# First two batches of an attention-and-MLP kernel: a new order, priced decoding, banks of their own for pooled values

## Chip, core and metric

The kernel runs on one core of one Trainium2 chip, in one launch. The metric is the device time of that launch in microseconds (us), lower is better. The engines are PE (matrix multiply, TensorE), DVE (VectorE), ACT (ScalarE), POOL (GpSimd) and SP, whose queue starts the transfers.

## What is computed

Eight batches j of eight heads, 576 tokens of 64 values each. Every head gets two attentions, and their sum goes through a layer that takes the maximum of three products:

```python
q_d, k_d, v_d = (t.reshape(B, H, 144, 4, 64).mean(axis=3) for t in (q, k, v))
out_up = np.repeat(sm_attn(q_d, k_d, v_d), 4, axis=2)      # pooled, every row repeated 4 times
scores = np.where(np.abs(i - j) < 4, scale * q @ k.T, -1e9)  # local
out_local = softmax(scores) @ v
x = (out_up + out_local)            # as 4608 tokens x 512
h = max(x @ w1, x @ w2, x @ w3)     # 512 -> 768
out = h @ w_out                     # 768 -> 512
```

q, k, v are float32, the weights are float64.

## The kernel before, in words

**Units of work.** A batch is a block j; n = 2j and 2j+1 are its halves of four heads (two pairs each). What of the 144 pooled positions goes beyond 128 is kept apart for all batches and makes a ninth block. A block's way: local and pooled attention give x, transposed (features on the partitions) in four tiles of 128x512, one per pair of heads; `transposes(j, c)` splits each into xhi (fp32r, cast by ACT) and xlo = x - xhi (DVE). `mlp_column(j, ft)` makes 128 of the 768 hidden values: 3 weights x 4 tiles x 3 products (xhi*whi, xhi*wlo, xlo*whi), 36 matmuls of 512 columns into three banks; then the maximum, then `mlp_out`. Blocks 2 to 7 do their local attention on DVE, POOL and ACT (products prod<-k,pq, sums of 1792 values, x<-pv).

**The first two batches.** Nothing can be multiplied by the weights until the first x is there. `dense(0)` and `dense(1)` therefore compute batches 0 and 1 by banded matmuls on PE: `band_load`, `wide_scores` or `band_scores`, softmax on ACT and DVE, `wide_values` or `band_values` (into banks given by PX), `band_sums` (pooled q and k), `pool_scores`, and `pooled_values`. ORDER names these steps in the order in which they are recorded: a letter (l load q and k, w load v, s scores, k pooled sums, v values, P pooled scores and softmax, V pooled values), then the half n, then the pair where it has one. FIRST, POOLED and PULL are their priorities.

**IN_PSUM.** Where it is True for n, the local values stay in their PSUM bank (stop=False) and `pooled_values` adds the pooled product onto them there. Since one pooled row is for four tokens, the moving operand is read four times: matmuls of 64x512, and of 64x16 for the rest. Then xhi is cast from the bank and xlo subtracted from it. Where it is False, `band_done` copies the local values to the tile x, the pooled product goes into a bank of its own as 64x144, ACT copies it to od, and `transposes` adds the two on DVE into t (t<-x,od) before the cast and the subtraction:

```python
elif c in blk["band"]:
    xs = new([P, FAC * P], tag="t", bufs=3, name=f"xs_{j}_{c}")
    tt(xs..., blk["band"][c], od, ALU.add)
    act.copy(hi, xs)
    tt(lo, xs, hi.bitcast(F32), ALU.subtract)
```

Before, batch 0 (n=0 and 1) is summed in PSUM, batch 1 takes the way just quoted.

**Weights.** `weight_piece` fetches one of 24 pieces of 128x512 float64 (524 KB) raw into the tile that STAGE or STAGE_OUT names for it (tiles that are otherwise wo, hh or pv), and decodes it in four steps: a cast to 16 bit of the top part (hqk<-hh, hqk<-wo or hqk<-pv, on ACT or DVE), SCALAR_TENSOR_TENSOR on DVE (shift and or, in place), whi (or the hi half of wo) by a cast on ACT, and wlo = value - whi on DVE or POOL. Three pieces serve one MLP column.

**The order.** All calls are recorded by `Recorder.add`; `place` is a list scheduler that keeps a model of each engine's time. `price` gives each call's duration, and the constants LAG, LAG0, MLP, PE_LAG, BANK_LAG, HOP, LOAD, SPARE and PATIENCE_DVE give what it adds for hand-overs, due times and choices between engines. Calls that two engines can do (`tt`, `copy`) go where the model has them done earlier. Each engine's queue is then emitted in that fixed order at one line, L639 (L643 after the change), so all instructions carry this line and are told apart by their tiles. Where the model has PE waiting up to the time KEEP_TO, `warm` puts fillers in: matmuls with the constant tile prod as both operands, 128x448 bf16, into a bank that is free (KEEP_UP and GUARD decide how densely).

Of the kernel before, what the change touches and what calls it, by code (L numbers as in the profile page):

```python
# [15 lines left out]
HALF = (BF16, F16, U16)  # L16
# [22 lines left out]
QW2 = D - 6  # L39
NW2 = 9  # L40
QT2 = NW2 * QW2
EXPS = (1, 2, 0, 2)
GEO = ("wide", "small")
EPS = 1e-9
QS = 1.0 / 128.0
QB = 1.0 / 8.0
XBUFS = 5
LAG = 317.941
LAG0 = 109.942
MLP = 2180.474  # L50
PE_LAG = 2614.299
BANK_LAG = 2600.0
SEG = FAC * P
NDENSE = 2
FIRST = (13.78, -82.74, 12.12, 93.98)
DENSE_SPARE = 182.496
POOLED = (-29.04, -8.81, 69.1, 12.11)
IN_PSUM = (True, True, False, False)
PULL = (-884.46, -2751.93, 13232.89, 22753.07)
PX = (['pq', 'pm'], ['pm', 'pm'], ['pq', 'pa'], ['pa', 'pa'])  # L60
VHOMES = ('k', 'pv', 'wlo4', 'whi4')
HOMES = ('whi2', 'whi3', 'whi2', 'pv', 'whi5', 'whi5', 'wlo4', 'wlo4')
STAGE = ('hh3', 'hh1', 'wo4', 'hh4', 'pv', 'hh3', 'wo5', 'wo5', 'wo4', 'pv', 'hh4', 'wo0', 'hh4', 'wo1', 'wo0', 'pv', 'hh5', 'hh4')
STAGE_OUT = ('hh4', 'hh1', 'hh0', 'hh5', 'hh4', 'hh5')
ALIGNED = ("prod", "pv", "hqk", "hv", "pd", "pt", "qkT", "k", "v", "q", "qd", "kd", "traw", "vd", "tq", "th")
JOINT = 0
JOINT_LAG = 3170.373
W_ENGINES = ("POOL",)
S_ENGINES = ("DVE",)
C_ENGINES = ("DVE",)  # L70
# [27 lines left out]

ENGINES = ("PE", "DVE", "ACT", "POOL", "SP")
DONE_NS = {"PE": 230.0, "DVE": 150.0, "ACT": 190.0, "POOL": 200.0}  # L100
SPARE = 1994.467
PATIENCE_DVE = 187.71
PATIENCE = {"PE": 0.0, "DVE": 142.18, "ACT": 0.0, "POOL": 0.0, "SP": 0.0}
LANES = 8
RING = 128
# [6 lines left out]
PHASE = 2200.0  # L112
KEEP = 0.352
EASY = 0.0
ORDER = ('l0 s00 k00 l1 w1 k01 w0 s01 v01 v00 k10 s11 s10 k11 v10 v11 P0 V0 P1 V1', 'l0 k00 s0 w0 v0 l1 k01 k10 w1 k11 s1 v1 P0 V0 P1 V1')
TAGS = ('pm', 'pm', 'pa', 'pa')
GUARD = 0.015
KEEP_UP = 0.137
KEEP_TO = 53544.303
HOP = 684.824  # L120
STEP = 451.011
LOAD = 8107.482
SWITCH = {("R", "P"): 120.0, ("P", "R"): 110.0, ("P", "T"): 25.0, ("T", "P"): 93.0, ("t", "P"): 90.0, ("P", "t"): 90.0, ("B", "P"): 96.0, ("M", "P"): 100.0, ("P", "M"): 20.0, ("R", "T"): 10.0, ("T", "R"): 5.0, ("R", "M"): 91.0, ("T", "M"): 93.0, ("M", "R"): 300.0, ("M", "T"): 305.0, ("M", "B"): 0.0, ("B", "M"): 96.0, ("B", "R"): 120.0, ("t", "R"): 90.0, ("R", "t"): 95.0, ("t", "M"): 90.0, ("t", "B"): 90.0, ("t", "T"): 90.0, ("T", "t"): 90.0, ("M", "t"): 100.0}
COLD = 1.9

# [109 lines left out]
class Recorder:  # L235
# [48 lines left out]
    def add(self, forms):  # L284
# [17 lines left out]
        o.group = self.step + next(iter(forms))[:2]  # L302
        if "PE" in forms and self.lag in (LAG, MLP):
            o.lag, o.margin = PE_LAG, BANK_LAG
        elif self.lag == MLP:
            o.lag = 0.0
# [27 lines left out]
    def price(self, eng, method, args, kw):  # L334

        out = kw["out"] if "out" in kw else args[0]
        n = elems(out)
        src = [a for a in args[0 if "out" in kw else 1 :] if is_ap(a)] + [v for k, v in kw.items() if is_ap(v) and k not in ("out", "accum_out")]
# [30 lines left out]
        if eng == "DVE":  # L369
            if method == "memset":  # L370
                return 60.0 + 0.3 * n, False
            if method == "transpose":
                return 100.0 + 1.045 * n, False
            if method == "tensor_reduce":
                return 66.0 + 1.045 * elems(src[0]), False
            if method in ("tensor_scalar", "tensor_scalar_mul", "tensor_scalar_add", "reciprocal", "tensor_copy"):
                fast = not any(psum) and not self.psum(out)
                return (125.0 if method == "reciprocal" else 140.0 if n == TAIL else 72.0) + n * (0.53 if fast else 1.045), fast and method != "reciprocal"
            return (185.0 if n == HH * NO * FAC else 62.0) + 1.045 * n, big >= 2
        if eng == "ACT":  # L380
            if n <= D and list(out.ap)[0][1] == D and any(psum):
                return 165.0 + 0.9 * n, False
            return 0.833 * n + (58.0 if any(psum) else 100.0) + 90.0 * ptrs + (93.0 if "accum_out" in kw else 0.0), False
        if eng == "POOL":
            if method == "memset":
# [265 lines left out]
def local_global_attention_maxout_kernel(ctx: ExitStack, tc: tile.TileContext, q, k, v, qt_dense, kt_dense, qt_pool, kt_pool, qkt_tail, v_win0, v_win1, v_tail, w_in, w_out, ident_d, mask_d, band_d, out):  # L651
# [463 lines left out]
    def wide_scores(n, pr, tag):  # L1115
# [16 lines left out]
        for i in range(2):  # L1132
            part = sm[:, :, i]
            if i < EXPS[n]:
                dve.tensor_reduce(out=mx[:, i], in_=sps[i], axis=AX.X, op=ALU.max, negate=True)
# [107 lines left out]
    def pair_operands():  # L1243
# [17 lines left out]
        for c in range(NCC):  # L1261
# [3 lines left out]
            for f in range(FAC):  # L1265
                pe.transpose(ps[:, f], x[:, f], ident)
            rec.lag = LAG
            tag, bufs = (("hv", 1), ("pt", 1), ("x", XBUFS), ("x", XBUFS))[c]
# [195 lines left out]
    def block(j):  # L1464
        rec.spare = SPARE
        for n in (2 * j, 2 * j + 1):
            with at(100.0 * n, LAG):
                attention(n)
        rec.spare = 0.0

    def turn(j):
        with at(-200.0, LAG0 if j < 2 else LAG):
            for c in range(NCC):
# [16 lines left out]
    for j in range(B + 1):  # L1490
# [8 lines left out]
        if 6 < n < 2 * B:  # L1499
            rec.spare = SPARE  # L1500
            with at(100.0 * n, LAG):
                begin(n)
# [3 lines left out]
    state["blk", B]["h"] = [None] * NFT  # L1506
    with at(100.0 * 2 * (B + 1), LAG):
        xt = pair_operands()
    with at(-100.0, MLP):
        joint_in(xt)  # L1510
# [52 lines left out]
```

## Time and profile before

| | us |
|---|---|
| median of 3 runs (lowest, highest) | 703.22 (702.65, 704.92) |
| the profiled execution | 701.49 |
| its span, first to last instruction | 699.7 |
| PE busy | 690.2 (99%) |
| DVE busy | 611.5 (87%) |
| ACT busy | 417.2 (60%) |
| POOL busy | 376.9 (54%) |

How to read it: the span lies 1.8 us below the profiled execution's own time, and that lies 1.7 below the median. A matmul's busy time overlaps that of its neighbours (a 128x512 lasts 0.39 us alone and comes every 0.23 in a row), so on PE the distance from start to start counts. The same holds, less strongly, for ACT and DVE. A filler counts as PE work. The wait in brackets in a timeline is the engine's idle time ahead of that instruction, with the instruction or transfer that ended it.

### The profile page before, as it was taken

Reading aid. Unit: us, or ns where it says so; the run is one execution under the profiler, and the core shown is the slowest. Engines: PE = TensorE matmul, PEld = TensorE weight load, DVE = VectorE, ACT = ScalarE, POOL = GpSimd, SP = SyncE. Lnnn points to the kernel's source line nnn. Section 1 sums busy time; section 2 is a strip of 40 time slices with the busy share of each in tenths; the row PEclk is TensorE's granted clock in tenths of the full one; section 3 lists DMA queues with packets and bytes.
Section 4 is the critical chain, followed back from the end, with each engine's and each line's share of the span. In section 5 each row is a group of like instructions: output and inputs, shape, how many; then the busy total and the mean of one; then the engine's idle time right before and its main releaser. Section 6 shows DMA issues by size and latency. Waiting matters only on the chain.

```text
span 699.7 us, 12779 instructions
## 1 busy us (share of the span) xinstructions
PE 690.2 (99%) x4350; PEld 547.8 (78%) x4350; DVE 611.5 (87%) x842; ACT 417.2 (60%) x1423; POOL 376.9 (54%) x590
## 2 busy tenths in 40 slices
PE   7999999999999999999999999999999999999997
PEld 4567887787887888778877887788788888888885
DVE  7987989999999999999999999999976398999620
ACT  5844466769578587857867665864866244334121
POOL 2102006899498888957757993975667013422000
PEclk9999999999999999999999999999999999999999
DMA  9994345765455555645374444441420010000012
GB/s 314 401 341 154 109 142 160 229 199 160 145 183 169 156 159 172 199 146 174 94 224 125 136 151 150 130 138 47 141 71 2 0 46 16 0 1 0 1 61 60
DMA packets 50180, 92.81 MB, mean 133 GB/s; under 512 B 5540, under 2 KB 19426, under 8 KB 50114
## 3 DMA queue, kind: packets, MB, share of 16 engines
q1 hardware_dynamic: 50114, 91.99, 41.7%
q8 instruction: 34, 0.56, 0.3%
q14 instruction: 32, 0.26, 0.1%
HBM read 82.53 MB, written 9.44 MB: 131 GB/s over the span
## 4 chain that ended last, share of the span: by engine, by line
PE 97%; DMA 1%; ACT 1%; DVE 0%; issue 0%; SPq 0%; ACTq 0%; DVEq 0%
PE pm L639 81%; PE pa L639 14%; PE pq L639 2%; DMA whi<-in_kt_dense_dram 1%; ACT pv L639 0%; SPq L639 0%; ACT y L639 0%; DVE xlo_0r L639 0%; DVE hh_0r L639 0%; DVE pa L639 0%; ACT xhi_0r L639 0%; ACT pd L639 0%; ACT dtail L639 0%; ACTq L1559 0%; DVE pdt L639 0%
## 5 line engine op out<-in xcount | busy, mean ns | idle before, releaser
L639 PE MATMUL pm<-xhi_0r,whi_0r 128*128 128x512 f32 x540 | 212.4, 394 | 0.0
L639 PE MATMUL pm<-xlo_0r,whi_0r 128*128 128x512 f32 x540 | 211.7, 393 | 0.0
L639 PE MATMUL pm<-xhi_0r,wlo_0r 128*128 128x512 f32 x540 | 211.6, 392 | 0.0
L639 ACT ACTIVATE pv<-v,sums 128x64 f32<-128x64 f32 x580 | 151.7, 413 | 22.5 <-POOL sums L639 10.4
L639 POOL TENSOR_TENSOR pv<-v,sums 128x256 f32<-128x256 f32 x233 | 138.7, 702 | 11.4 <-DVE x L639 8.7
L639 PE MATMUL pm<-wo_0r,hh_0r 128*128 128x512 f32 x576 | 138.7, 394 | 0.0
L639 PEld LDWEIGHTS pm<-wo_0r,hh_0r 128*128 128x128 f32 x576 | 106.6, 188 | 22.5 <-issue 1.3
L639 PEld LDWEIGHTS pm<-xhi_0r,whi_0r 128*128 128x128 f32 x540 | 101.5, 188 | 21.5 <-issue 1.1
L639 PEld LDWEIGHTS pm<-xlo_0r,whi_0r 128*128 128x128 f32 x540 | 101.4, 188 | 21.3 <-issue 0.7
L639 PEld LDWEIGHTS pm<-xhi_0r,wlo_0r 128*128 128x128 f32 x540 | 101.4, 188 | 21.0 <-issue 0.4
L639 DVE TENSOR_TENSOR prod<-k,pq 128x1792 f32<-128x1792 f32 x56 | 112.2, 2004 | 2.1 <-PE pa L639 1.8
L639 DVE TENSOR_REDUCE sums<-prod 128x28 f32<-128x1792 f32 x56 | 112.2, 2004 | 0.5
L639 DVE TENSOR_REDUCE x<-pv 128x256 f32<-128x1792 f32 x36 | 72.2, 2009 | 2.9 <-POOL pv L639 1.7
L639 POOL TENSOR_TENSOR pv<-pv 128x768 f32<-128x768 f32 (+1 forms) x40 | 62.2, 1555 | 3.6 <-ACT pv L639 1.8
L639 POOL TENSOR_TENSOR x<-whi_0r,wlo_0r 128x512 f32<-128x512 f32 x16 | 22.4, 1410 | 55.3 <-DVE x L639 28.4
L639 ACT COPY y<-pm 128x512 f32<-128x512 f32 (+1 forms) x50 | 28.9, 583 | 37.0 <-PE pm L639 32.9
L639 ACT CAST hh_0r<-pm 128x512 fp32r<-128x512 f32 x47 | 27.7, 589 | 38.8 <-DVE pm L639 37.8
L639 POOL TENSOR_TENSOR hv<-v 128x128 f32<-128x128 f32 (+1 forms) x52 | 25.1, 498 | 27.7 <-DMA v<-in_v_dram 13.0
L639 DVE TENSOR_TENSOR t<-pm,t 128x512 f32<-128x512 f32 x43 | 29.3, 680 | 10.4 <-PE pm L639 10.1
L639 ACT COPY pq<-q 128x256 f32<-128x256 f32 x56 | 22.1, 396 | 26.2 <-DVE prod L639 22.0
L639 DVE TENSOR_TENSOR pm<-pm,t 128x512 f32<-128x512 f32 x44 | 30.4, 690 | 4.9 <-PE pm L639 4.8
L639 DVE TENSOR_TENSOR hh_0r<-pm,hh_0r 128x512 fp32r<-128x512 f32 x47 | 31.9, 679 | 2.2 <-ACT hh_0r L639 2.0
(381 smaller groups left out, 1052.9 us busy)
## 6 DMA issues: line engine op xcount, KB each, us to landing
k<-in_k_dram SPq DMA_DIRECT2D x55, 320.0 KB
v<-in_v_dram SPq DMA_DIRECT2D x54, 320.0 KB
out_dram<-y SPq DMA_DIRECT2D x35, 256.0 KB
q<-in_q_dram SPq DMA_DIRECT2D x56, 128.0 KB
hqk<-in_qt_pool_dram SPq DMA_DIRECT2D x24, 256.0 KB
hqk<-in_kt_pool_dram SPq DMA_DIRECT2D x24, 256.0 KB
hh<-in_w_in_dram SPq DMA_DIRECT2D x8, 511.8 KB
wo<-in_w_in_dram SPq DMA_DIRECT2D x7, 511.8 KB
```

The costliest lines, as they stand in the source:

```text
L639: getattr(self.engines[o.eng], method)(*map(real, args), **{k: real(x) for k, x in kw.items()})
```

## The change

It gives all halves of batches 0 and 1 banks of their own for the pooled product (IN_PSUM all False), other banks for batch 1 (PX), a new order of the steps of `dense`, other tiles for nine of the raw weight pieces, new priorities and planner constants, and three durations in `price`: casts to 16 bit cost 452 ns on DVE and 785 on ACT, and a cast from every second word (the whi cast) 667 on ACT, where the general formula gave some 343, 526 and 526. KEEP_TO ends the fillers at 43.3 us of the planner's time, not 53.5. EXPS is only read for n = 0 and 1, so its third number changes nothing.

```diff
-EXPS = (1, 2, 0, 2)
+EXPS = (1, 2, 1, 2)
-LAG = 317.941
-LAG0 = 109.942
-MLP = 2180.474
-PE_LAG = 2614.299
-BANK_LAG = 2600.0
+LAG = 398.26
+LAG0 = -62.603
+MLP = 470.841
+PE_LAG = 2645.417
+BANK_LAG = 2923.268
-FIRST = (13.78, -82.74, 12.12, 93.98)
-DENSE_SPARE = 182.496
-POOLED = (-29.04, -8.81, 69.1, 12.11)
-IN_PSUM = (True, True, False, False)
-PULL = (-884.46, -2751.93, 13232.89, 22753.07)
-PX = (['pq', 'pm'], ['pm', 'pm'], ['pq', 'pa'], ['pa', 'pa'])
+FIRST = (3.52, -159.77, 86.5, 242.04)
+DENSE_SPARE = 120.777
+POOLED = (-24.14, 55.55, 39.95, 55.59)
+IN_PSUM = (False, False, False, False)
+PULL = (-3705.32, -1193.36, 7524.09, 14455.02)
+PX = (['pq', 'pm'], ['pm', 'pm'], ['pa', 'pa'], ['pq', 'pa'])
-STAGE = ('hh3', 'hh1', 'wo4', 'hh4', 'pv', 'hh3', 'wo5', 'wo5', 'wo4', 'pv', 'hh4', 'wo0', 'hh4', 'wo1', 'wo0', 'pv', 'hh5', 'hh4')
-STAGE_OUT = ('hh4', 'hh1', 'hh0', 'hh5', 'hh4', 'hh5')
+STAGE = ('wo4', 'hh1', 'wo4', 'hh3', 'pv', 'pv', 'wo5', 'wo5', 'wo4', 'pv', 'hh4', 'wo0', 'hh4', 'wo1', 'wo0', 'pv', 'wo0', 'hh4')
+STAGE_OUT = ('wo5', 'hh5', 'pv', 'hh1', 'hh4', 'hh4')
-JOINT_LAG = 3170.373
+JOINT_LAG = 3815.887
...
-SPARE = 1994.467
-PATIENCE_DVE = 187.71
+SPARE = 1758.738
+PATIENCE_DVE = 164.439
...
-ORDER = ('l0 s00 k00 l1 w1 k01 w0 s01 v01 v00 k10 s11 s10 k11 v10 v11 P0 V0 P1 V1', 'l0 k00 s0 w0 v0 l1 k01 k10 w1 k11 s1 v1 P0 V0 P1 V1')
+ORDER = ('l0 l1 w0 k00 s00 w1 s01 v01 k01 k10 v00 s11 k11 P0 s10 v10 v11 V0 P1 V1', 'l0 s0 w0 v0 k00 l1 k10 k01 k11 s1 w1 v1 P0 V0 P1 V1')
-GUARD = 0.015
-KEEP_UP = 0.137
-KEEP_TO = 53544.303
-HOP = 684.824
+GUARD = -0.005
+KEEP_UP = 0.087
+KEEP_TO = 43349.76
+HOP = 772.772
-LOAD = 8107.482
+LOAD = 5244.941
...
             if method in ("tensor_scalar", "tensor_scalar_mul", "tensor_scalar_add", "reciprocal", "tensor_copy"):
                 fast = not any(psum) and not self.psum(out)
+                if out.dtype in HALF:
+                    return 452.0, True
                 return (125.0 if method == "reciprocal" else 140.0 if n == TAIL else 72.0) + n * (0.53 if fast else 1.045), fast and method != "reciprocal"
         if eng == "ACT":
             if n <= D and list(out.ap)[0][1] == D and any(psum):
                 return 165.0 + 0.9 * n, False
+            if out.dtype in HALF or src[0].ap[-1][0] == 2:
+                return 785.0 if out.dtype in HALF else 667.0, False
             return 0.833 * n + (58.0 if any(psum) else 100.0) + 90.0 * ptrs + (93.0 if "accum_out" in kw else 0.0), False
```

In the tables below, pm, pa and pq are PSUM banks, pt and ptt the transposed pooled probabilities, vd and vs the pooled v, and xhi_0r to wlo_0r the split operands of the MLP.

PE before, inside the first MLP column (27 of its 36 matmuls stand above these rows):

```order
L639 MATMUL pm_197<-xlo_0r,whi_0r 128x512
L639 MATMUL pm_160<-pt_154,vd_513 64x512 x2
L639 MATMUL pm_160<-ptt_399,vs_557 64x512 x2
L639 LDWEIGHTS prod_121
L639 MATMUL pa_162<-prod_121 128x448
...
L639 MATMUL pa_162<-prod_121 128x448
L639 MATMUL pm_168<-xhi_0r,whi_0r 128x512
L639 MATMUL pm_168<-xhi_0r,wlo_0r 128x512
```

PE after, the last products before the MLP:

```order
L643 MATMUL pa_226<-pt_154,vd_472 64x144 x2
L643 MATMUL pa_158<-pt_154,vd_472 64x144 x2
L643 MATMUL pa_226<-ptt_368,vs_528 64x144 x2
L643 MATMUL pa_158<-ptt_368,vs_528 64x144 x2
...
L643 MATMUL pa_234<-prod_121 128x320
L643 MATMUL pm_156<-y_383,pv_264 64x58 x16
...
L643 MATMUL pa_234<-whi_0_142 26x32
L643 MATMUL pa_226<-whi_0_142 26x32
L643 MATMUL pm_170<-xhi_0r,whi_0r 128x512
L643 MATMUL pm_170<-xhi_0r,wlo_0r 128x512
L643 MATMUL pm_170<-xlo_0r,whi_0r 128x512
```

The pooled values of n=1 have moved from inside the first column to a place ahead of it, in eight-fold packs of 64x144 in two banks; between the last of these rows and the column's end no pooled product and no filler stands.

DVE before, the decoding ahead of the last xlo of batch 0 (last row; 10 casts, 12 SCALAR_TENSOR_TENSOR and 12 wlo in all from the start to here):

```order
L639 CAST hqk_131<-wo_0_276 128x512
...
L639 SCALAR_TENSOR_TENSOR wo_0_276<-wo_0_276,hqk_131 128x512
...
L639 SCALAR_TENSOR_TENSOR hh_0_251<-hh_0_251,hqk_136 128x512
L639 TENSOR_TENSOR wlo_0r<-wo_0_276,whi_0r 128x512
L639 TENSOR_TENSOR wlo_0r<-hh_0_251,whi_0r 128x512
L639 CAST hqk_131<-hh_0_284 128x512
L639 SCALAR_TENSOR_TENSOR hh_0_284<-hh_0_284,hqk_131 128x512
L639 TENSOR_TENSOR xlo_0r<-pm_160,xhi_0r 128x512
```

DVE after, the same place (5 casts, 4 SCALAR_TENSOR_TENSOR and 4 wlo from the start to here):

```order
L643 TENSOR_TENSOR wlo_0r<-hh_0_285,whi_0r 128x512
L643 CAST hqk_134<-wo_0_247 128x512
L643 SCALAR_TENSOR_TENSOR wo_0_247<-wo_0_247,hqk_134 128x512
L643 TENSOR_TENSOR t_682<-x_605,od_480 128x512
L643 CAST hqk_134<-pv_129 128x512
L643 TENSOR_TENSOR wlo_0r<-wo_0_247,whi_0r 128x512
L643 TENSOR_TENSOR t_492<-x_727,od_480 128x512
L643 TENSOR_TENSOR xlo_0r<-t_682,xhi_0r 128x512
L643 TENSOR_TENSOR wlo_0r<-hh_0_315,whi_0r 128x512
L643 TENSOR_TENSOR xlo_0r<-t_492,xhi_0r 128x512
```

Eight of the twelve decoded pieces have gone behind the last xlo, and two of the four adds t<-x,od of batch 0 stand in these rows in their place. On ACT, 4 whi casts stand ahead of the last xhi cast where there were 11, no hqk cast where there were 2, and 4 copies x and 8 copies od are new there. Over the whole program PE has 48 fillers in place of 90, DVE 39 sums x<-pv in place of 36, POOL 17 in place of 20.

## Rows read from the trace of the kernel before

**Rows 1.** page, parts 1 and 2: busy time per engine; DVE's busy tenths in 40 slices

```profile
PE 690.2 (99%) x4350; PEld 547.8 (78%) x4350; DVE 611.5 (87%) x842; ACT 417.2 (60%) x1423; POOL 376.9 (54%) x590
...
DVE  7987989999999999999999999999976398999620
```

**Rows 2.** page, part 4: the chain that ended last, by engine

```profile
PE 97%; DMA 1%; ACT 1%; DVE 0%; issue 0%; SPq 0%; ACTq 0%; DVEq 0%
```

**Rows 3.** PE's timeline, 43 to 60 us: start us, us, engine, operation, count

```profile
43.05 0.41 PE L639 MATMUL pa<-pt,vd 128*64 128x16 f32 x6
...
47.30 0.50 PE L639 MATMUL pm<-xhi_0r,whi_0r 128*128 128x512 f32 x1
...
53.65 1.08 PE L639 MATMUL pm<-pt,vd 128*64 128x512 f32 x4
...
54.66 1.07 PE L639 MATMUL pm<-ptt,vs 32*64 32x512 f32 x4
...
55.67 1.12 PE L639 MATMUL pa<-prod 128*128 128x448 bf16 x5
...
59.91 0.40 PE L639 MATMUL pm<-xhi_0r,whi_0r 128*128 128x512 f32 x1
```

**Rows 4.** ACT's timeline, 40 to 57 us; brackets: idle us before, and the releaser

```profile
40.49 0.67 ACT L639 CAST whi_0r<-hh 128x512 fp32r<-128x512 f32 x1
...
41.06 0.26 ACT L639 COPY ptt<-pa 128x128 f32<-128x128 f32 x1
...
55.78 0.58 ACT L639 CAST xhi_0r<-pm 128x512 fp32r<-128x512 f32 x1 [5.57 <-PE pm L639]
...
56.26 0.79 ACT L639 CAST hqk<-hh 128x512 f16<-128x512 bf16 x1
```

**Rows 5.** DVE's timeline, 49 to 58 us

```profile
49.76 0.46 DVE L639 CAST hqk<-wo 128x512 f16<-128x512 bf16 x1
...
50.11 0.41 DVE L639 TENSOR_TENSOR vd<-hv 128x256 f32<-128x256 f32 x1
...
50.44 0.68 DVE L639 SCALAR_TENSOR_TENSOR wo<-wo,hqk 128x512 uint32<-128x512 uint32 x1
...
51.04 0.68 DVE L639 TENSOR_TENSOR wlo_0r<-pv,whi_0r 128x512 fp32r<-128x512 f32 x1
...
57.60 0.69 DVE L639 TENSOR_TENSOR wlo_0r<-wo,whi_0r 128x512 fp32r<-128x512 f32 x1 [4.69 <-ACT whi_0r L639]
```

**Rows 6.** PE's timeline, 285 us: pooled values of a later block

```profile
284.95 0.71 PE L639 MATMUL pa<-pt,vd 128*64 128x144 f32 x8
...
285.59 0.47 PE L639 MATMUL pa<-ptt,vs 32*64 32x144 f32 x8
```

**Rows 7.** windows: stretch, then PE, PEld, DVE, ACT, POOL busy, clock, DMA share, GB/s

```profile
0.00:20.00 20.00, 16.11 (x184) 9.48 (x184) 15.90 (x52) 11.14 (x50) 4.17 (x13) 1.00 0.93 323
...
8.60:43.17 34.57, 34.38 (x367) 19.32 (x365) 31.55 (x82) 27.33 (x123) 6.25 (x13) 1.00 1.03 394
...
0.00:58.81 58.81, 54.73 (x708) 32.82 (x708) 45.98 (x119) 34.49 (x135) 9.66 (x23) 1.00 0.90 326
...
8.60:56.26 47.66, 47.47 (x542) 28.20 (x540) 40.08 (x100) 31.02 (x130) 7.53 (x16) 1.00 0.96 357
```

**Rows 8.** turns of blocks 3 and 6, DVE's and PE's timelines; DVE's group of pv sums

```profile
279.60 1.28 DVE L639 TENSOR_TENSOR xlo_0r<-pa,xhi_0r 128x512 fp32r<-128x512 f32 x2
...
288.53 0.39 PE L639 MATMUL pm<-xlo_0r,whi_0r 128*128 128x512 f32 x1
...
488.89 0.63 PE L639 MATMUL pa<-ident,x 128*128 128x128 f32 x4 [0.29 <-DVE xlo_0r L639]
...
L639 DVE TENSOR_REDUCE x<-pv 128x256 f32<-128x1792 f32 x36 | 72.2, 2009 | 2.9 <-POOL pv L639 1.7 <-ACT pv L639 1.2
```

**Rows 9.** PE's timeline, 5 to 9 us: the wide scores of two pairs of heads

```profile
5.53 1.32 PE L639 MATMUL pm<-whi 64*58 64x64 f32 x36 [0.51 <-DMA whi<-in_kt_dense_dram]
...
7.59 0.77 PE L639 MATMUL pm<-whi 64*58 64x64 f32 x36 [0.20 <-DMA whi<-in_kt_dense_dram]
```

## The prediction

> **What bounds the kernel now.** I read the busy line of the page first, then the chain of waits, then the windows of the first 60 us, then the timelines of the engines there. The busy line has PE at 690.2 of 699.7 us, DVE at 611.5, ACT and POOL far below [rows 1]. The chain that ended last is PE for 97% [rows 2]. So the time is PE's list: what PE executes, fillers included, plus its few waits. The busy share hides that the 90 fillers (the matmuls 128x448 and their like on the constant tile prod, put in where the planner expects PE to be idle) count as work. In program order 84 of them stand ahead of the first MLP matmul, at 47.30 us [rows 3]. From there PE only runs out of operands once in a visible way: after 27 MLP matmuls it does pooled values of n=1 (8 matmuls of 512 columns, 53.65 to 55.67), then five fillers, and only then is there an xhi of the last quarter of x to multiply [rows 3]. ACT had waited 5.57 us for just these products before it could cast them at 55.78 [rows 4], and DVE 4.69 us, to 57.60, for a whi cast that stood behind that one on ACT [rows 5]. The first column's 36 matmuls are through at 59.91, where the 37th starts [rows 3]; at 0.23 us each they need 8.2. So two things can be won ahead of 60 us: matmuls that need not be, and the idle time that fillers cover.
>
> **Products on PE.** Before, batch 0's pooled values are added onto the local values inside the same PSUM bank, so each half-batch n=0,1 repeats every pooled column four times: 16 matmuls of 512 columns and 16 of 16. A group of four of the first takes 1.01 us (53.65 to 54.66 to 55.67) [rows 3], six of the second 0.41 [rows 3]. Per half-batch that is 4 x 1.01 + 16 x 0.41/6 = 5.1, less some overlap of neighbours; I take 4.9, 9.8 for both. In their place come eight 64x144 on 128 rows and eight on 32 rows per half-batch, as all other batches have: 0.64 (284.95 to 285.59) and at most 0.47 [rows 6], 1.1 together, 2.2 for both. Net **-7.6 us** of PE work. All of it lies on the path, since PE bounds.
>
> **What replaces the sum in PSUM.** Batch 0 now has four copies of x out of PSUM and eight of the pooled result od on ACT, and four adds t<-x,od on DVE, before its xhi casts and xlo subtractions. Copies: 0.5 us (the xhi cast, the same shape from PSUM, is 0.58 [rows 4]; neighbours overlap by some 0.1) and 0.2 (ptt<-pa 128x128, 0.26 [rows 4]), 4 x 0.5 + 8 x 0.2 = 3.6 us of ACT. Adds: 0.6 each as the other 512-column forms [rows 5], 2.4 us of DVE.
>
> **Decoding moved behind the start.** Up to the last xlo of batch 0, DVE's program had 10 casts hqk, 12 shift-and-or, 12 wlo; it has 5, 4 and 4. From start to start these last 0.35, 0.60 and 0.60 us (49.76, 50.11; 50.44, 51.04; the wlo at 51.04 has the duration of the shift-and-or) [rows 5]: 5 x 0.35 + 8 x 0.60 + 8 x 0.60 = 11.35 us less ahead of that xlo. ACT has 7 whi casts and 2 hqk casts fewer ahead of the last xhi: 7 x 0.57 + 2 x 0.7 = 5.4 us (40.49 to 41.06; 0.79 less overlap) [rows 4]. None of this work is gone: it is done later, while PE runs MLP columns, and must not hold those.
>
> **When the first column can run.** DVE: 45.98 us busy to 58.81 [rows 7], -11.35 + 2.4 = 37.0 us of work. Its waits there are 12.83, of which 4.69 are the wait above, that goes with the cause; 4.1 of the rest fall in the first 20 us (15.90 busy) [rows 7] and come from the first loads. The last xlo is then done between 37.0 + 4.1 = 41.1 and 37.0 + 8.1 = 45.1. ACT: nothing of weight before 8.60; 31.02 busy from there to 56.26 [rows 7], -5.4 + 3.6 = 29.2; its waits from 8.60 to 43.17 were 7.2 [rows 7]; so the last cast ends between 37.8 and 45.0, and the subtraction on DVE 1.2 later: 39.0 to 46.2. The middles, 43.1 and 42.6; I take **43.0**, ends 39 and 46. In the new order some 12 matmuls of the first bank come before one that needs this xlo, so the first MLP matmul can start 12 x 0.23 = 2.7 earlier, at 40.3. Then 36 x 0.23 + 0.9 (the band products of the second half-batch of batch 1, which PE does inside) end the first column at 49.4, against 59.91: **10.5 us** earlier (7.5 to 14.5). As a check: 7.6 are the products, 2.9 fillers and waits, of which 42 fillers fewer (90 to 48 in program order, 0.2 us each: five in 1.12 [rows 3]) are 8, so that PE's own waits may grow by 5.
>
> **Loads.** The new order and homes put the third piece of the first column behind 10.0 MB (5.5 before). At 394 GB/s [rows 7] that is 26 us, near 28 with the start; its decoding is four steps of at most 0.7, so it is there 9 us ahead. The piece nearest to being late is the third of the second column: its home comes free only just before the first MLP matmul, and I estimate its wlo at 54 against a need at 55. If that slips by 1 or 2 us the gain loses as much; I put it at nothing and leave it in the range. POOL takes 17 multiplies pv from ACT over the whole program; both engines are idle for over 40% [rows 1], and DVE's sums of pv stay the later step, so I cost it at nothing.
>
> **What is given back.** With PE 10.5 earlier, DVE's lead over it shrinks. At the turn of block 3 the third xlo is ready at 280.9 and PE first wants it at 288.53: 7.6 us [rows 8]. At the turn of block 6 PE already waits 0.29 for DVE [rows 8]. DVE gains too: at the last xlo of batch 0 it is 58.9 - 43.0 = 15.9 earlier with 11.35 of decoding put off, so 4.5 ahead. Lead at block 3: 7.6 - 10.5 + 4.5 = 1.6, less what DVE gets on top later: up to 4 adds for batch 1 (2.4) and three more reduces x<-pv of 2.0 us [rows 8] that POOL did before. If a third of that 8.4 falls ahead of the tight turns, PE stalls for about 1; with all of it, 6.8. At block 6, with no lead at all, the stall has the same two ends. I take **2.5**, nearer to the row with a lead, because most turns have it. Sum: -10.5 + 2.5 = -8.0, from 701.49 (the profiled run, span 699.7) to 693.5. The profiled run is 1.7 below the median of 703.22, so the forecast on the median is **695.2**.
>
> **Rivals.**
> (a) DVE takes over as the bound at the turns: all 8.4 us of added DVE work ahead of them, stall 6.8, net -3.7, **699.5**. For it: DVE is near full from 100 to 500 us [rows 1], and 611.5 grows by some 11. Against: the leads at the other turns, and MLP columns that PE can do meanwhile.
> (b) The start stays where it was because loads set it. DMA is full (share 1.03, 394 GB/s) to 43.17 [rows 7]. If the first column needs all of what landed by 45 us, it ends at 45 + 8.2 + 0.9 = 54.1, gain 5.8, less 2.5: **699.9**. Against: the piece that counts is at 28 us.
> (c) The change's saving is taken back whole, fillers turned into plain waits and later stalls as in (a) on a start as in (b): within 2 us of **703.2**.
> (d) Slower: PE's clock. The granted clock stands at 1.00 (2.4 GHz) in all those windows [rows 7], but the same 36 wide-score matmuls took 1.32 us at 5.53 and 0.77 at 7.59 [rows 9]: the first matmuls, after an idle PE, run at the lower level (1.2 GHz), 1.7 times as long. 42 of the fillers that kept PE at work go. If in the new gaps the clock falls, each us of PE work lasts 0.7 us more. To eat 8.0 us and 2.1 of measurement, 10.1/0.7 = 14 us of work must run at the low level, half of what PE has ahead of 40 us (some 19 useful, 9 fillers). Place: 10 to 40 us. Price then **705.5**. Against: 48 fillers stay, spread over just these gaps, and ACT and DVE have to be on the path with all of it. The Trainium skill ("TensorE: Matmul & The Clock Gate", section "What's actually happening") says that the slow level is the default and that activity releases it, which is the rule that speaks against taking fillers out; by it the loss would be up to the 705.5 of this rival. The pair of rows at 5.53 and 7.59 agrees with it; no row here shows a fall in the middle of a program.
>
> **Chances.** Forecast (690 to 698.5) 0.60; better than 690 (both ends of the start, no stall) 0.07; (a) and (b) together 0.19; (c) 0.07; (d) 0.07. A difference under 0.3%, 2.1 us, can't be told from no change here. Faster by more: 0.60 + 0.07 + most of (a) and (b), 0.83. Same: 0.09. Slower: 0.08. The range takes the early start with little stall, -14.5 + 0.8, as its low end, 689.5, and (a), (b) with a late piece as its high end, 701.5. The forecast alone is 690 to 698.5.
>
> **What would show it.** The first MLP matmul near 40 and the 37th near 49.5; no pooled values with 512 columns; no wait of ACT or DVE of 4 us or more between 40 and 60; 48 fillers; a wide-score or score matmul after 10 us at its fast duration; PE waits on DVE at some turns, 1 to 4 us in all. A first MLP matmul at 45 or later makes the start wrong; PE waits of 6 us at the turns make (a) right; matmul durations of 1.7 times make (d) right.

## The result and the profile after

Faster, near the forecast: 695.14 us (median of 4 runs, 693.87 to 697.99) against 703.37 for the kernel before, a ratio of 0.9886 [0.9851, 0.9920]. The same kernel measured again beside the last experiments gave 693.16 (692.38 to 693.83), a ratio of 0.9853 [0.9836, 0.9870]. The forecast was 695.2, its range 689.5 to 701.5. The profiled execution took 695.34, 6.15 less than that of before; its span is 693.6. The profiled execution of before lies 1.9 below its median and that of the changed kernel 0.2 above its own, so a comparison of the two profiles shows some 2 us less than the medians do.

The page of the changed kernel: busy time by engine, DVE's tenths in 40 slices, the chain that ended last.

```profile
PE 677.1 (98%) x4276; PEld 543.5 (78%) x4276; DVE 622.8 (90%) x856; ACT 399.1 (58%) x1361; POOL 375.8 (54%) x597
...
DVE  7989889999999999999999998999989898999720
...
PE 89%; DVE 5%; DMA 2%; ACT 1%; issue 1%; SPq 0%; ACTq 0%
```

Against [rows 1, 2]: PE has 13.1 us less to do (products and fillers), DVE 11.3 more, and PE's share of the chain is 89% in place of 97%. The chain's longest pieces off PE lie ahead of 33 us (ACT and DVE), at 64.2 (a load of 6.6 us), from 95 to 117 (DVE and a load, while PE does not wait) and from 615 to 634 (DVE): the start now hangs on ACT and DVE too, and two of the waits below are in it.

PE's timeline where the first column begins and ends.

```profile
34.86 0.71 PE L643 MATMUL pa<-pt,vd 128*64 128x144 f32 x8
...
38.40 0.50 PE L643 MATMUL pm<-xhi_0r,whi_0r 128*128 128x512 f32 x1
...
46.69 0.39 PE L643 MATMUL pm<-xhi_0r,whi_0r 128*128 128x512 f32 x1
...
47.47 0.87 PE L643 MATMUL pa<-whi 64*26 64x32 f32 x80
...
48.27 0.50 PE L643 MATMUL pm<-xhi_0r,whi_0r 128*128 128x512 f32 x1
```

The first MLP matmul is at 38.40, 8.9 us earlier than in [rows 3]. The pooled values of n=1 stand ahead of it as packs of eight (34.86, and those on 32 rows 0.64 later). The 37th MLP matmul starts at 46.69. The banded products of batch 1's second pair come behind the 39th, so like is compared with like at 48.27 less three matmuls of 0.23: 47.6 against 59.91, 12.3 us earlier.

Windows up to the last xlo of batch 0 and of a stretch behind it (columns as in [rows 7]), and that xlo on DVE's timeline.

```profile
8.60:39.53 30.93, 28.72 (x462) 19.17 (x455) 29.39 (x81) 28.14 (x130) 5.89 (x11) 1.00 1.03 383
0.00:40.68 40.68, 33.75 (x532) 22.83 (x533) 35.15 (x99) 29.62 (x132) 6.66 (x16) 1.00 0.97 353
85.00:90.00 5.00, 5.00 (x22) 3.57 (x21) 4.79 (x9) 1.74 (x4) 0.00 (x0) 0.67 0.78 221
```

```profile
40.00 0.68 DVE L643 TENSOR_TENSOR xlo_0r<-t,xhi_0r 128x512 fp32r<-128x512 f32 x1
```

DVE works 35.15 us up to the end of that xlo at 40.68, and waits 5.53. ACT works 28.14 from 8.60 to the last xhi cast's end at 39.53, and waits 2.8.

PE's timeline where the lead of 12.3 us gets lost again: four places behind the first column. DVE's row for the sum that the first of them waits for comes last.

```profile
71.66 1.00 PE L643 MATMUL pa<-wlo 64*26 64x32 f32 x80 [1.57 <-DVE qkT L643]
...
83.64 0.76 PE L643 MATMUL pa<-qkT 64*128 64x144 f32 x7 [0.85 <-issue]
...
85.35 0.63 PE L643 MATMUL pm<-xhi_0r,wlo_0r 128*128 128x512 f32 x1
...
85.78 0.63 PE L643 MATMUL pm<-xlo_0r,whi_0r 128*128 128x512 f32 x1
...
88.31 0.40 PE L643 MATMUL pm<-xlo_0r,whi_0r 128*128 128x512 f32 x1
```

```profile
633.65 0.50 PE L643 MATMUL pq<-prod_0r,wlo_0r 128*128 128x512 f32 x1 [1.74 <-DVE whi_0r L643]
```

```profile
70.87 0.69 DVE L643 TENSOR_REDUCE qkT<-wlo 128x128 f32<-128x512 f32 x1 [1.20 <-DMA wlo<-in_qt_dense_dram]
```

PE waits 1.57 us at 71.66 for sums of q and k of batch 1's last pair, for which DVE itself waits 1.20 for the load of q; then 0.85 at 83.64 for nothing that the profile names, and 1.74 at 633.65 for a sum of DVE in the last two blocks. From 85.35 to 88.31 the matmuls of 512 columns come every 0.43 us: seven steps take 2.96 in place of 1.59, 1.4 us more, and the granted clock of 85 to 90 is 0.67, so for some of it TensorE stood at its lower level (1.2 GHz); PE had done small matmuls of 26 columns and the wait of 0.85 before. These four make 5.6 of the 6.2 us between 12.3 and the 6.15 that are left. The starts of the same MLP matmuls (an xhi or xlo with whi_0r or wlo_0r, counted in order of time) in both kernels bear it out. The 253rd and the 1201st, before and then changed:

```profile
143.71 0.39 PE L639 MATMUL pm<-xhi_0r,whi_0r 128*128 128x512 f32 x1
...
462.37 0.39 PE L639 MATMUL pm<-xhi_0r,whi_0r 128*128 128x512 f32 x1
```

```profile
135.48 0.39 PE L643 MATMUL pm<-xhi_0r,whi_0r 128*128 128x512 f32 x1
...
454.32 0.39 PE L643 MATMUL pm<-xhi_0r,whi_0r 128*128 128x512 f32 x1
```

The changed kernel is 8.2 us ahead at the first and 8.1 at the second, and still 8.2 at the 1601st (639.55 and 631.30). So 4.1 us are lost ahead of 136 us, nothing over the turns of blocks 2 to 5, and 2.1 behind 631.

### The profile page after: what moved, and what is told of

Read it like the earlier page. It is cut to its first block, busy times and chain, and to the rows that moved or that the text cites. A ratio compares the mean times of both kernels' runs of the same rounds, so it can differ in the third digit from the quotient of the medians.

```text
span 693.6 us, 12574 instructions
## 1 busy us (share of the span) xinstructions
PE 677.1 (98%) x4276; PEld 543.5 (78%) x4276; DVE 622.8 (90%) x856; ACT 399.1 (58%) x1361; POOL 375.8 (54%) x597
## 4 chain that ended last, share of the span: by engine, by line
PE 89%; DVE 5%; DMA 2%; ACT 1%; issue 1%; SPq 0%; ACTq 0%
PE pm L643 75%; PE pa L643 12%; PE pq L643 2%; DMA wlo<-in_qt_dense_dram 1%; DVE prod L643 1%; DMA whi<-in_kt_dense_dram 1%; DMA pt<-in_v_tail_dram 1%; ACT prod L643 1%; DVE odtail L643 1%; DVE x L643 0%; DVE t L643 0%; DVE pm L643 0%; DVE xlo_0r L643 0%; DVE sums L643 0%; ACT pa L643 0%
## 5 line engine op out<-in xcount | busy, mean ns | idle before, releaser
L643 POOL TENSOR_TENSOR pv<-v,sums 128x256 f32<-128x256 f32 x250 | 148.3, 704 | 7.9 <-DVE x L643 5.0
L643 ACT ACTIVATE pv<-v,sums 128x64 f32<-128x64 f32 x512 | 134.5, 412 | 28.2 <-DVE x L643 12.5
L643 DVE TENSOR_REDUCE x<-pv 128x256 f32<-128x1792 f32 x39 | 78.1, 2009 | 2.0 <-ACT pv L643 2.0
L643 POOL TENSOR_TENSOR pv<-pv 128x768 f32<-128x768 f32 (+1 forms) x34 | 52.9, 1557 | 1.8 <-ACT pv L643 0.3
L643 ACT CAST hh_0r<-pm 128x512 fp32r<-128x512 f32 x47 | 27.7, 588 | 43.0 <-DVE pm L643 42.2
L643 POOL TENSOR_TENSOR x<-whi_0r,wlo_0r 128x512 f32<-128x512 f32 x16 | 23.5, 1471 | 49.8 <-DVE x L643 33.0
L643 POOL TENSOR_TENSOR qd<-hqk 128x256 f32<-128x256 f32 x24 | 17.9, 744 | 32.2 <-DMA hqk<-in_qt_pool_dram 32.1
L643 DVE TENSOR_TENSOR t<-pm,t 128x512 f32<-128x512 f32 x43 | 29.2, 679 | 4.0 <-PE pm L643 3.9
```

Source lines behind the costliest of these rows:

```text
L643: getattr(self.engines[o.eng], method)(*map(real, args), **{k: real(x) for k, x in kw.items()})
```

## The experiments

All ratios are to the kernel before, run on the same chip. "Fixed order" means that the changed kernel's planned order is kept and only the named instructions are touched; in the other kernels the planner orders all anew. Lines added in a kernel shift the line number of its rows. The rounds of experiments ran on three chips (the kernel before took 703.4, 704.2 and 703.7 there), so times of different rounds compare by their ratios. Fillers are counted in the traces by their 128x448 form.

| kernel | us (median) | ratio [95%] | first MLP matmul | last xlo of batch 0 ends | fillers |
|---|---|---|---|---|---|
| before | 703.4 | | 47.30 | 58.9 | 90 |
| changed | 695.14 | 0.9886 [0.9851, 0.9920] | 38.40 | 40.7 | 48 |
| changed, again | 693.16 | 0.9853 [0.9836, 0.9870] | 39.12 | 41.4 | 48 |
| a_inpsum | 704.99 | 1.0018 [1.0004, 1.0032] | 48.81 | 50.1 | 27 |
| b_banks | 701.42 | 0.9963 [0.9946, 0.9979] | 46.73 | 49.8 | 18 |
| b_banksprice | 702.85 | 0.9987 [0.9975, 1.0000] | 46.41 | 50.6 | 15 |
| a_oldprice | 700.13 | 0.9937 [0.9915, 0.9959] | 37.22 | 41.2 | 47 |
| a_products4 | 701.16 | 0.9964 [0.9948, 0.9979] | 44.90 | 47.2 | 48 |
| a_lo5 | 709.10 | 1.0062 [1.0038, 1.0086] | 40.92 | 51.8 | 48 |
| a_nofill | 695.03 | 0.9873 [0.9853, 0.9894] | 40.30 | 42.2 | 0 |
| a_loadfirst | 694.06 | 0.9859 [0.9837, 0.9882] | 39.49 | 41.8 | 48 |
| a_joint | 692.37 | 0.9836 [0.9815, 0.9856] | 39.26 | 41.5 | 48 |
| a_best | 691.78 | 0.9838 [0.9821, 0.9855] | 38.94 | 41.2 | 48 |
| a_bestfill | 691.36 | 0.9830 [0.9811, 0.9848] | 38.81 | 41.1 | 48 |

The control:

> The changed kernel once more, as it is, as the measure for the three beside it: 694 to 696.

693.16, just below what was expected. Two measurements of one kernel lie 2 us apart, so of what follows only differences above that are taken as shown, unless the trace shows the wait that goes or comes.

**Banks undone, and banks alone.**

```diff
-IN_PSUM = (False, False, False, False)
+IN_PSUM = (True, True, False, False)
```

> The changed kernel with one line undone: batch 0's pooled values are again summed in the PSUM bank of the local values, and the planner orders all anew. Theory 1 (the products are PE work on the path, 7.6 us): some 5 to 8 us above the changed kernel's 695.1, so 700 to 703. Theory 2 (the new order and prices bring the gain, products hide beside the waits that fillers cover, and ACT and DVE even save 6 us of copies and adds): within 2 us of 695.

The same line the other way round, in the kernel before:

> The kernel before with that line alone changed: banks of their own for batch 0's pooled values, old order constants, old prices, old homes. Theory 1: most of the gain, 695 to 698. Theory 2: little, 701 to 704. If both parts are needed together, between: about 699.

The changed kernel without its banks is at 704.99, as slow as before and above the 700 to 703 of theory 1; the kernel before with the banks gains 0.4%, theory 2's number. Neither theory holds as it was put: without the banks there is no gain, and alone they bring 2.0 us, a fifth to a quarter of it. One reservation goes for this and the next two experiments: the planner makes a new plan each time, with constants that were set for another kernel, and the number of fillers changes with it (last column). So these runs show what each kernel does, not the price of one part by itself. What goes wrong in each is in the traces. PE of a_inpsum around its longest wait:

```profile
29.72 0.45 PE L643 MATMUL pa<-qkT 64*32 64x144 f32 x8
...
36.42 0.45 PE L643 MATMUL pm<-ident,prod 128*128 128x128 f32 x1 [6.26 <-DVE prod L643]
```

PE stands 6.26 us for a probability tile of DVE. Its column starts at 48.81, later than before. In b_banks two windows of PE (busy, granted clock, DMA share, GB/s):

```profile
10.00:20.00 10.00, 5.92 (x53) 0.75 1.03 395
30.00:40.00 10.00, 5.30 (x43) 0.60 1.03 404
```

PE is idle for 8.8 of these 20 us, and does a part of its work at the lower clock. DVE still has nine wlo ahead of the last xlo (twelve before, four in the changed kernel), which ends at 49.8: what is taken off PE, products and fillers, turns into waits, and how much of the loss is the clock without those fillers was not separated.

**Banks and prices, with the old order.**

```diff
-IN_PSUM = (True, True, False, False)
+IN_PSUM = (False, False, False, False)
...
+                if out.dtype in HALF:
+                    return 452.0, True
...
+            if out.dtype in HALF or src[0].ap[-1][0] == 2:
+                return 785.0 if out.dtype in HALF else 667.0, False
```

> The kernel before with banks of its own for batch 0 and with the three prices, its constants, order string and homes kept. In program order 8 wlo subtractions still stand ahead of the last xlo of batch 0, twice as many as in the changed kernel. If decoding ahead of it sets the start, it stays late (46 or more for the first MLP matmul) and the time is 699 to 702. If banks and prices are the change and the rest is tuning, 695 to 697.

702.85, no gain worth the name, a little above the upper end that this case gave. Windows of PE:

```profile
10.00:20.00 10.00, 5.81 (x47) 0.74 1.03 396
30.00:40.00 10.00, 5.94 (x40) 0.59 1.04 397
```

The same picture as with the banks alone: 8.2 us idle of 20, the clock at 0.74 and 0.59, the last xlo at 50.6. Banks and prices are not enough; with the new order, constants and homes the banks pay. Which of these three does it was not taken apart.

**The new order without the prices.** The changed kernel less the two rules of the diff's last part.

```diff
-                if out.dtype in HALF:
-                    return 452.0, True
...
-            if out.dtype in HALF or src[0].ap[-1][0] == 2:
-                return 785.0 if out.dtype in HALF else 667.0, False
```

> The changed kernel without the two rules that price the decoding's casts; its constants, order string, banks and homes stay, and the planner orders all anew. If the prices matter by themselves (casts taken for 0.1 to 0.26 us shorter than they are, so PE work is placed for operands that are late), there are PE waits of 2 us or more ahead of 40 us, and the time is 698 to 702. If the constants and the order string carry the gain, 694 to 697.

700.13, as for prices that matter, but not at the place that was expected: the first MLP matmul comes at 37.22, earlier than with them. The loss lies behind it. Windows of PE:

```profile
60.00:80.00 20.00, 18.83 (x379) 0.91 0.45 157
80.00:100.00 20.00, 17.95 (x228) 0.83 0.32 104
64.50:67.80 3.30, 3.23 (x9) 0.50 0.93 349
85.00:91.70 6.70, 6.22 (x59) 0.50 0.47 167
```

and two of PE's rows:

```profile
64.57 0.42 PE L639 MATMUL pa<-prod 128*128 128x320 bf16 x1 [1.17 <-issue]
...
86.89 1.33 PE L639 MATMUL pa<-qkT 64*128 64x144 f32 x7 [0.48 <-issue]
```

From 60 to 100 us PE is idle for 3.2 us, and for 10 us of it the granted clock is 0.50 (1.2 GHz); the 145th MLP matmul starts at 88.2 against 84.7 and 84.3 in the two profiles of the changed kernel. Ten us at half pace can cost up to 5 (an estimate from these windows), which is all that this kernel lacks, and the longest wait there, 1.17 us, names no operand at all. So the run shows that this plan is slower; that it is so because casts are late is not shown, and no wait was traced to a cast.

**The products four times, in fixed order.**

```diff
-        rec.add({"PE": value_products(n, po)})
+        rec.add({"PE": value_products(n, po)}).again = 4 if n < 2 else 1
```

> The changed kernel in its own fixed order, with the pooled products of n=0 and n=1 done four times over (same result): 3 x 1.05 us more PE work for each, 6.3 in all, nothing else moved. Theory 1 (PE's list is the path ahead of the first MLP matmul): first MLP matmul 5 to 6 us later than 38.4, time 700 to 701.5. Theory 2 (ACT and DVE set the start): under 2 us more, 695 to 697.

PE at the products of n=1 and at the first MLP matmul:

```profile
38.22 0.71 PE L643 MATMUL pa<-pt,vd 128*64 128x144 f32 x8
...
39.26 0.71 PE L643 MATMUL pa<-pt,vd 128*64 128x144 f32 x8
...
44.90 0.50 PE L643 MATMUL pm<-xhi_0r,whi_0r 128*128 128x512 f32 x1
```

Each set takes 1.04 us (38.22 to 39.26), the first MLP matmul comes 6.5 later than 38.40, and the time is 6.0 above 695.1 (8.0 above the control). Theory 1 holds inside the changed kernel: PE's list up to the first MLP matmul is on the path, us for us.

**The wlo subtractions five times, in fixed order.**

```diff
+            if o.eng == "DVE" and o.group.startswith("weights") and o.forms["DVE"][0][0] == "tensor_tensor":
+                o.again = 5
```

> The changed kernel in its own fixed order, with the four wlo subtractions that stand ahead of the last xlo of batch 0 done five times each (same result): 16 x 0.6 = 9.6 us more DVE work ahead of that xlo. If decoding ahead of the xlo is on the path, as my sum of DVE's work up to it says, the xlo and the first column come 7 to 9.6 us later and the time is 701 to 704. If PE's own list sets the start, under 3 us more: 695 to 698.

709.1, 14 above the changed kernel, more than the 9.6 that were added and than the 704 that was expected (its profiled execution took 706.5, 11 above). DVE's timeline, and PE's windows there:

```profile
47.57 3.59 DVE L647 TENSOR_TENSOR wlo_0r<-hh,whi_0r 128x512 fp32r<-128x512 f32 x5
...
51.08 0.68 DVE L647 TENSOR_TENSOR xlo_0r<-t,xhi_0r 128x512 fp32r<-128x512 f32 x1
```

```profile
40.00:50.00 10.00, 5.60 (x94) 0.77 0.67 211
50.00:60.00 10.00, 8.39 (x63) 0.72 0.49 157
```

Five subtractions take 3.59 us, so 0.60 each. The last xlo ends 11.1 later than in the changed kernel, PE waits 3.22 and 1.61 for xlo inside the column, and the clock falls to 0.77 and 0.72, which stretches what it then does. DVE's list ahead of that xlo is on the path too, and beyond its own length, since PE's waits cost clock.

**No fillers, in fixed order.** The 48 fillers are left out.

```diff
-        out = self.place()
+        out = [o for o in self.place() if o.eng != "PE" or not o.forms["PE"][0][1][0].tensor.name.startswith("fill_")]
```

> The changed kernel in its own fixed order without any of its 48 fillers. If fillers hold PE's clock up (the rival of a falling clock), some stretch between 10 and 40 us has a granted clock below 1.00 and matmuls at nearly twice their step, and the time is 5 to 10 us above 695: 700 to 705. If they only stand in waits, the time is the same within 1 us and the waits show as PE idle. If they stand on the path themselves, since a fixed order executes them even where PE is late, the first MLP matmul comes 1 to 3 us earlier than 38.4 and the time is 692 to 694.

695.03: the same time, but by none of the three mechanisms alone. PE at its two longest waits in the first 40 us that no load ended, and at the first MLP matmul; a window of PE:

```profile
13.90 1.39 PE L643 MATMUL pm<-ident,prod 128*128 128x128 f32 x5 [2.99 <-ACT pa L643]
...
15.75 1.96 PE L643 MATMUL pm<-y,k 64*64 64x58 f32 x32 [0.46 <-ACT y L643]
...
29.46 1.34 PE L643 MATMUL pm<-ident,prod 128*128 128x128 f32 x5 [3.36 <-ACT pa L643]
...
31.26 1.97 PE L643 MATMUL pm<-y,pv 64*64 64x58 f32 x32 [0.46 <-ACT y L643]
...
40.30 0.50 PE L643 MATMUL pm<-xhi_0r,whi_0r 128*128 128x512 f32 x1
```

```profile
30.00:36.00 6.00, 5.49 (x50) 0.50 1.04 395
```

Without fillers the granted clock is 0.50 from 30 to 36 us: TensorE runs at 1.2 GHz after a stand of 3.36 us, and the 32 small matmuls at 31.26 take 1.97 us (1.14 with fillers). That is the rival of a falling clock, seen at its full depth. The 32 small matmuls of the same size at 15.75 take just as long, 1.96 us (1.14 at 15.78 with fillers), so PE was at the lower level there too, although the granted clock reads 1.00 in windows ahead of 19 us. It costs 1.9 us at the first MLP matmul (40.30 against 38.40; 1.2 against the control). The Trainium skill ("TensorE: Matmul & The Clock Gate", section "What's actually happening") calls the slow level the default that activity releases; this window agrees. Its price is far below the 5 to 10 us that were expected. My reading, not tested, is that most of what PE does slowly here lies beside ACT's and DVE's work.

**Loads first, in fixed order.**

```diff
+        late = [o for o in out if dst(o) in ("rawin_5_0", "rawin_4_0")]
+        out = [o for o in out if o not in late]
+        k = max(k for k, o in enumerate(out) if dst(o) == "bandqk_3_1") + 1
+        out[k:k] = late
```

> The changed kernel in its own fixed order, with the two raw weight pieces of the fifth and sixth column (2 x 524 KB) fetched behind, not ahead of, q and k of the last pair of batch 1. PE waited 1.57 us at 71.7 for sums of those q and k, whose load was in flight from 64.2 to 70.9 at 300 GB/s. If this load is what ended the wait, the wait goes (1 MB less ahead of it is 3 us) and nothing else waits, since the fifth column starts at 84: 693.5. If DVE was late with the sums for its own work, no change: 695. If the pieces come late, a wait before the fifth column takes its place: 695 or more.

What PE waited for in it (total us, times, longest; the last three of 0.8 us or more):

```profile
PE pq L648 <- DVE whi_0r L648: 1.7, 1, 1.7
PE pa L648 <- issue: 0.9, 1, 0.9
PE pa L648 <- DMA wlo<-in_kt_dense_dram: 0.8, 1, 0.8
```

The wait for the sums qkT is gone, a wait of 0.8 for the other pair's k, at 65.3, is new, and nothing waits before the fifth column. But this does not show that the moved pieces did it: in a_joint (next) the loads are in their old order and the wait is gone as well, with one of 1.18 at 65.42 in place of it. That a load ended the wait where it occurs stands on DVE's row at 70.87 in the changed kernel. 694.06 lies between the two measurements of the changed kernel, so a shorter time is not shown either.

**JOINT_LAG as before.**

```diff
-JOINT_LAG = 3815.887
+JOINT_LAG = 3170.373
```

> The changed kernel with one constant of the last two blocks, JOINT_LAG, as it was before (3170 in place of 3816); only the order behind 490 us differs. PE waited 1.74 us at 633.7 for a DVE sum there, and the kernel before had no such wait. If this constant made it, the wait goes and the time is about 693.5. If it comes from DVE's being full between 600 and 650 us, a wait of 1 to 2 us stays and the time is 695.

Two of its waits ahead of 500 us, where its order is that of the changed kernel:

```profile
65.42 0.89 PE L643 MATMUL pa<-wlo 64*26 64x32 f32 x80 [1.18 <-DMA wlo<-in_kt_dense_dram]
...
274.19 0.66 PE L643 MATMUL pa<-ident,pd 128*128 128x128 f32 x4 [1.07 <-DVE xlo_0r L643]
```

The wait of 1.7 for whi_0r in the last two blocks is gone, and the time is 692.37, 2.8 below the first and 0.8 below the second measurement of the changed kernel. The constant made that wait: all eight profiles with the new value have it (1.7 us), none of the six with the old one has. Its price is as steady. From the start of the 1601st MLP matmul to the end of the span it is 62.2 us in each of those eight and 60.2 in each of those six (within 0.1), so the new JOINT_LAG costs 2.0 us in every profile; the medians, 2 us apart for one kernel, can't show it.

**Both, and both with a cover.** a_best has the two diffs above together; a_bestfill adds seven idle matmuls behind the burst of small ones (its diff stands below).

> The changed kernel with both repairs: the two raw pieces fetched behind q and k of the last pair, and JOINT_LAG as before. The waits at 71.7 and 633.7 lie at different places of PE's list, so if both repairs are real they add up: 1.1 and 2.8 below the changed kernel, 691 to 692. If the first was noise, 692.4 as with JOINT_LAG alone.

691.78 (690.87 to 692.74), 1.4 below the control beside it (692.38 to 693.83), not the 3.9 that the two differences made added up: both were taken against the slower of the two measurements. Its trace has neither wait. By its ratio (0.9838) it is no faster than a_joint (0.9836), so the moved loads add nothing that can be told.

```diff
+                    for _ in range(7):
+                        self.engines["PE"].matmul(real(full), real(mlp[1][1]), real(mlp[1][2][:, : 2 * SD]), start=True, stop=True, skip_group_check=True)
```

> The same with seven matmuls of 288 columns (0.9 us) behind the 78 small ones of the last banded values at about 82 us, where PE stood 0.85 us for nothing the profile shows and the granted clock fell to 0.67 behind it in one profile. If the small matmuls let the clock fall and the stand is hidden by the seven, 0.5 to 2 us below the kernel without them. If neither comes often, 0 to 0.9 us above it.

691.36, within 0.5 of the kernel without them. The stand without a named cause has moved along with the program:

```profile
82.05 0.95 PE L656 MATMUL pa<-xhi_0r,wlo_0r 128*128 128x288 f32 x6 [0.57 <-issue]
```

Now it follows the first of the seven inserted matmuls (six are left in this row), still 0.57 us. So it isn't the pooled scores that wait; it comes at the same count of PE's instructions, whatever stands there (more on this at the end). The clock stayed at 1.00 there, but it did so in the control as well. This is the fastest kernel of the study: 1.8 us below the control and 3.8 below the first measurement of the changed kernel, though its interval and the control's still overlap by a tenth of a per cent.

## Why the prediction was right, and which step was not

**Products.** -7.6 us on PE, all on the path. In the new order this holds: 6.3 us put back cost 6.0 to 8.0. As a price of the banks by themselves it does not: alone they brought 2.0 (b_banks), where PE waits for DVE and ACT instead, with 18 fillers in place of 90. The prediction saw that fillers hide in the busy share, and still took all of the 7.6 as lying on the path.

**Decoding behind the start.** DVE's sum of 37.0 us of work and 4.1 to 8.1 of waits was 35.15 and 5.53; ACT's 29.2 and up to 7.2 was 28.14 and 2.8. The last xlo was forecast for 43.0 and came at 40.7, inside 39 to 46, because DVE had 1.9 less to do than summed and ACT's waits fell from 7.2 to 2.8. The step is sound and a_lo5 shows its weight: work put back ahead of that xlo costs its length and more.

**Start.** Forecast 40.3 for the first MLP matmul and 10.5 us gained by the end of the first column; measured 38.40 and 12.3. The sum was 1.8 too careful.

**Loads.** The third piece of the second column, feared late, held nothing: the second column starts without a wait. The load that did hold PE was another, q and k of batch 1's last pair behind 1 MB of weights (71.66, by DVE's row at 70.87).

**What is given back.** This is the step that failed: "If a third of that 8.4 falls ahead of the tight turns, PE stalls for about 1; with all of it, 6.8 [...] I take 2.5". DVE's lead did shrink. At the turn of block 3, DVE's timeline, then PE's:

```profile
279.33 1.27 DVE L643 TENSOR_TENSOR xlo_0r<-pa,xhi_0r 128x512 fp32r<-128x512 f32 x2
```

```profile
274.04 0.39 PE L643 MATMUL pm<-xhi_0r,whi_0r 128*128 128x512 f32 x1
...
277.91 0.61 PE L643 MATMUL pm<-xhi_0r,whi_0r 128*128 128x512 f32 x2
```

The last two xlo are ready at about 280.0 and 280.6, nearly as late as before (280.3 and 280.9; the prediction took the second of these for the third xlo, which makes DVE's lead 8.2 and not 7.6), while PE begins the column at 274.04, so little of that lead is left. But nothing stalls: where the kernel before has every third matmul an xlo, the new order puts six of xhi in a row from 277.91. PE is busy for 199.8 of the 200 us from 100 to 300, and for all of those from 300 to 500, and what the changed kernel is ahead of the one before at the same MLP matmul falls only from 8.2 to 8.1 between 135 and 454 us. Priced at 2.5, the turns cost 0.1 to 0.2 in this pair. They are near their edge, though: in a_joint, with the same order up to there, PE waits 1.07 us for an xlo at 274.19, at this very turn. What was lost instead are 5.6 us elsewhere, which the sum had at nothing: 1.57 by a load, 0.85 by a stand that names no cause, 1.4 by the clock and 1.74 by JOINT_LAG. So in the profiled pair the start gave 1.8 more than forecast and 3.65 more was given back: 8.0 was forecast, 6.15 measured.

**How much of it was luck.** That the median came out at 695.14 against 695.2 is luck in part. Two terms were off in opposite directions, and the profiled execution, forecast at 693.5, took 695.34: only the 1.7 us that the forecast added from profile to median, where the measured median lies 0.2 below the profile, brings the two together. The medians, 8.2 the first time and 10.5 in the second, lie around the forecast also because three of the four losses change from one execution to the next: the control's profile has 0.73, 0.56 and none at 85 us of them, but again 1.73 by JOINT_LAG.

**Rivals.** (a), DVE as the bound at the turns: not seen in the changed kernel's two profiles; 1.07 us of it in a_joint. (b), loads setting the start: not seen, though a load held PE once later. (d), the clock: the mechanism is real (a_nofill 0.50, b_banks 0.60, a_lo5 0.72), and in the changed kernel it struck once in each profile. In the first it did at 85 us, for 1.4 us. In the second (the control) it did where the prediction had placed it, between 10 and 40 us, behind a wait of 1.94 for ACT:

```profile
13.50:16.80 3.30, 3.28 (x12) 0.50 1.03 395
```

Up to there the control was 0.35 us ahead of the first profile (13.52 against 13.87 for the same matmuls); the 32 score matmuls behind it start at 16.71 against 15.78, so the fall cost some 1.3. So the 48 fillers that are left do not keep the clock up in every execution.

## What to carry to other kernels

Taking work off the engine that is 99% busy paid here only where its operands came earlier too: the banks alone gave 0.4%, the new order with its prices alone nothing, both together 1.1 to 1.5%. Before a busy share is read as a bound, take out work that is only there to fill waits. Where a planner makes a new plan for each variant, a variant shows its own plan; an edit in the fixed order shows what one step costs. Count the other engines' work up to the operand that the busy one needs next, with waits between zero and those of before; that sum held here within 2.5 us. A lead that falls to zero is no stall yet where the order can put other work in between; look for what has no such freedom, the one load or sum that a whole group of matmuls needs.

## What the runs showed that was not expected

- A stand of 0.56 to 0.97 us on PE behind the last burst of small banded matmuls (at 82 to 84 us, in a_lo5 at 94), with no semaphore named: in the profiles of the changed kernel, its control, a_lo5, a_loadfirst, a_joint, a_best and a_bestfill, and of 0.48 in a_oldprice, and not in those of a_products4 and a_nofill, where other counts of instructions stand ahead. Counted in the traces (matmuls, weight loads and semaphore instructions of PE), it comes behind exactly 2497 instructions in all eight (a_inpsum has 0.24 there). Three other stands name no cause. They come behind 1729 instructions (a_oldprice, 1.17 us at 64.57), 961 (a_nofill, 0.16 at 40.13) and 1870 (b_banks, 0.17 at 78.13). All but the last of these counts are 193 plus 9, 6 or 3 times 256. The 256 instructions up to such a place, the stand included, take 2.9 to 3.6 us; between any other two of these counts PE takes 4.0 us or more, and no stand of this kind follows. So it comes where PE would get through 256 instructions faster than that, as it does in a burst of small matmuls, and the kernel's planner has just such a limit in its model (the class Fetch, at 193 and every 256 behind it). What the chip does there no trace shows.
- The cost of leaving out all 48 fillers, with TensorE at 1.2 GHz for six us from 30 on and, by its matmuls' durations, for the first 19, was 1.2 to 1.9 us at the first MLP matmul and nothing that can be told from the changed kernel at the end.
- A constant that works on the last two blocks alone (JOINT_LAG) made a wait of 1.7 us, and 2.0 us of time, in every profile that has its new value.
